# 96 dummy matmuls ahead of the first spectrum group, and two pieces of work moved from VectorE to ScalarE

**Chip, cores, metric.** The kernel runs on one core of a Trainium2 chip. The metric is the device time of one execution in microseconds (us); lower is better. Every run told of here was in the fast state: the granted clock was 0.998 to 1.0 throughout.

## The reference

Two layers alternate, A B A B, each in the form x + layer(layernorm(x)), on x of 2048 rows by 640 columns in bf16.

```python
def _A_ref(x, w_r, w_i):            # a filter in the spectrum
    X = rfft2(x.astype(float32))
    X = X * (w_r + 1j * w_i)
    return irfft2(X, s=(S, D)).astype(bfloat16)

def _B_ref(x, mem0, Wq, Wk, Wv, Wo, seg_len):   # 64 segments of 32 rows, 8 rows of memory carried on
    for s in range(n_seg):
        h = concatenate([mem, xs], axis=1)
        q, k, v = (einsum('btd,dhe->bhte', h, W) for W in (Wq, Wk, Wv))   # 32 heads of 128
        p = softmax(where(mask, einsum('bhqe,bhke->bhqk', q, k) * scale, -1e9))
        o = einsum('bhqk,bhke->bhqe', p, v)
        ...                                      # output projection; the first 8 rows become mem

x = x + _A_ref(_layernorm(x), A_w_r, A_w_i)
x = x + _B_ref(_layernorm(x), B_mem0, ...)
x = x + _A_ref(_layernorm(x), A_w_r, A_w_i)
x = x + _B_ref(_layernorm(x), B_mem0, ...)
```

## The kernel before

The change touches one function, which starts the first layer A from raw input. The 16 blocks of rows come in five loads and are worked on in five groups. For each row the moments are computed (on VectorE, or on ScalarE for rows 3, 7 and 11), then the row's factor (Ln and Exp on ScalarE, small operations on GpSimd). The layernorm isn't applied to the rows: the DFT table of the row is scaled instead. Then follow 60 matmuls a group (30 in the last two), five PSUM banks a group out of eight, and the evictions.

```python
groups = [(0, 4), (4, 8), (8, 12), (12, 14), (14, 16)]
by_act = (3, 7, 11)
pp = tc.alloc_tile_pool(name=f"{self.lname}_ps1", bufs=8, space=PSUM)

def act_stats(t):      # a row's moments on ScalarE
    nc.scalar.activation(out=scr[:, 0, :], in_=x[:, t, :], func=ACTF.Identity, scale=-D ** -1.5, accum_out=nm[:, t:t + 1])
    nc.scalar.activation(out=scr[:, 1, :], in_=x[:, t, :], func=ACTF.Square, scale=D ** -0.5, bias=nm[:, t:t + 1], accum_out=mv[:, t, 1:2])
...
def stats(t):          # the same on VectorE
    for hlf in range(2):
        nc.vector.bn_stats(out=st[:, t % 2, hlf, :], in_=x[:, t, hlf * 320:(hlf + 1) * 320])
    nc.vector.bn_aggr(out=mv[:, t, :], in_=st[:, t % 2, :, :])

def scale_tables(q):
    for t in range(*groups[q]):
        nc.vector.tensor_scalar_mul(out=Ts[:, t, :], in0=T[:, t, :], scalar1=rs[:, t:t + 1])
...
with tc.manual_schedule(...):      # every engine runs its part in the order written here
    ...
    empties(0, ps0, "  AAA")       # A: eviction on ScalarE, D: on VectorE
    for t in (12, 13):
        stats(t)
    scales(3)
    empties(1, ps1, "AA")
    scale_tables(2)
    ps2 = matmuls(2)
```

The reciprocals of the softmax sums go out to DRAM and come back broadcast to 128 partitions, two heads at a time. The value matmuls (`pso`) can run before that, but VectorE multiplies each finished bank by the broadcast (`Rb`) to empty it, and so frees the bank.

```python
def sums_back(h):
    ...
    nc.sync.dma_start(out=Rd[h][0:1, :].rearrange("o (g n) -> (o g) n", g=4), in_=R[0:128:32, :])
    if h % 2 or h == H - 2:
        for a in range(...):       # the pair's two heads
            nc.sync.dma_start(out=Rbs2[a % 2], in_=Rd[a][0:1, :].to_broadcast([128, 4 * NR]))

def value_group(h, P, Rb, oT, g_):
    pso = pa.tile([128, 512], FP32, name="pso", tag="pso")
    for ...:
        nc.tensor.matmul(pso[:, lo - q0:hi - q0], lhsT=V[...], rhs=P[...], ...)
    ...
    nc.vector.tensor_tensor(out=oT..., in0=byclass(po), in1=rx, op=ALU.mult)
    nc.vector.tensor_tensor(out=oTm[:, h, ...], in0=po[:, :, SEG], in1=rm, op=ALU.mult)
```

Of the kernel before, what the change touches and what calls it, by code (L numbers as in the profile page):

```python
# [10 lines left out]
FP32 = mybir.dt.float32  # L11
# [6 lines left out]
DRAM = bass.MemoryType.DRAM  # L18

S, D = 2048, 640  # L20
NF = 321
LN_EPS = 1e-5

# [171 lines left out]
class LayerA:  # L195
# [8 lines left out]
    def tables(self, gate=None, mirror=True):  # L204
        nc, cd = self.tc.nc, self.g["cd"]
        s5 = self.ar.get("S5", f"{self.lname}tab")
        self.Fd = s5.bf(5, 2, NF)
        self.K = s5.bf(19, 128)
        self.Wm = s5.bf(2, 7 * NF)
        self.wts = [s5.bf(2, NF) for _ in range(3)]  # L210
        self.W = {}
# [10 lines left out]
    def load_mirror(self, i):  # L222
        self.tc.nc.gpsimd.indirect_dma_start(out=self.Wm[:, i, :], out_offset=None, in_=self.w[i].rearrange("(p g) f -> p (g f)", g=16),
                                             in_offset=bass.IndirectOffsetOnAxis(ap=self.g["mirror"][:, 0:1], axis=0), element_offset=9 * NF)

    def load_w(self, p):
        nc, W, j = self.tc.nc, self.W, self.SEQ[p]
        W[j, 0] = self.wts[p % 3]
        if j:
            W[j, 1] = self.Wm[:, :, (7 - j) * NF:(8 - j) * NF]  # L230
        for i in range(2):
# [35 lines left out]
    def cold_raw(self, x_src, s3):  # L267




        nc, tc, g, x, T = self.tc.nc, self.tc, self.g, self.x, self.T
        Ts, scr = s3.bf(16, 128), s3.bf(2, D)
        mh = s3.bf(16, 2)
        st, mv = s3.f32(2, 2, nc.vector.BN_STATS_DIM), s3.f32(16, 2)
        nm, mn, rs, r0 = (s3.f32(16) for _ in range(4))
        for a, b in ((0, 2), (2, 4), (4, 8), (8, 12), (12, 16)):
            nc.sync.dma_start(out=x[:, a:b, :], in_=r16(x_src)[:, a:b, :])
            if a in (4, 8):
                nc.sync.dma_start(out=T[:, 2 * a - 8:2 * a, :], in_=g["cd"]["cT"][:, 2 * a - 8:2 * a, :])  # L280
        groups = [(0, 4), (4, 8), (8, 12), (12, 14), (14, 16)]
        by_act = (3, 7, 11)
        pp = tc.alloc_tile_pool(name=f"{self.lname}_ps1", bufs=8, space=PSUM)

        def act_stats(t):
            nc.scalar.activation(out=scr[:, 0, :], in_=x[:, t, :], func=ACTF.Identity, scale=-D ** -1.5, accum_out=nm[:, t:t + 1])
            nc.scalar.activation(out=scr[:, 1, :], in_=x[:, t, :], func=ACTF.Square, scale=D ** -0.5, bias=nm[:, t:t + 1], accum_out=mv[:, t, 1:2])

        def scales(q):
            a, b = groups[q]  # L290
            sl, v = slice(a, b), mv[:, a:b, 1]
            small = nc.gpsimd if q < 4 else nc.vector
            nc.scalar.activation(out=r0[:, sl], in_=v, func=ACTF.Ln, bias=g["eps"][:, 0:1])
            nc.scalar.activation(out=r0[:, sl], in_=r0[:, sl], func=ACTF.Exp, scale=-0.5)
            n = b - 1 if b - 1 in by_act else b
            small.tensor_scalar_mul(out=mn[:, a:n], in0=mv[:, a:n, 0], scalar1=-1.0)
            if n < b:
                small.tensor_scalar_mul(out=mn[:, n:b], in0=nm[:, n:b], scalar1=D ** 0.5)
            t, r = rs[:, sl], r0[:, sl]
            if small is nc.gpsimd:  # L300
                small.tensor_scalar_add(out=t, in0=v, scalar1=LN_EPS)
                small.tensor_tensor(out=t, in0=t, in1=r, op=ALU.mult)
            else:
                small.scalar_tensor_tensor(out=t, in0=v, scalar=LN_EPS, in1=r, op0=ALU.add, op1=ALU.mult)
            small.tensor_tensor(out=t, in0=t, in1=r, op=ALU.mult)
            small.tensor_scalar(out=t, in0=t, scalar1=-0.5, scalar2=1.5, op0=ALU.mult, op1=ALU.add)
            small.tensor_tensor(out=t, in0=t, in1=r, op=ALU.mult)
            small.tensor_copy(out=mh[:, sl, 0], in_=mn[:, sl])
            small.tensor_tensor(out=mh[:, sl, 1], in0=mn[:, sl], in1=mh[:, sl, 0], op=ALU.subtract)

        def stats(t):
# [3 lines that stand above are left out]

        def scale_tables(q):
            for t in range(*groups[q]):
                nc.vector.tensor_scalar_mul(out=Ts[:, t, :], in0=T[:, t, :], scalar1=rs[:, t:t + 1])

        def matmuls(q):  # L320
            a, b = groups[q]
            ps = {}

            def rows(ch):
                ps[ch] = pp.tile([128, 4, 128], FP32, name="ps1", tag="pa")
                for t in range(a, b):
                    nc.tensor.matmul(ps[ch][:, t - a, :], lhsT=x[:, t, ch * 128:(ch + 1) * 128], rhs=Ts[:, t, :], start=(t == a), stop=False)

            def means(ch):
                for t in range(a, b):  # L330
                    for i in range(2):
                        nc.tensor.matmul(ps[ch][:, t - a, :], lhsT=mh[:, t, i:i + 1].to_broadcast([128, 128]), rhs=Ts[:, t, :], start=False, stop=(i == 1 and t == b - 1))  # L332

            for ch in range(5):
                rows(ch)
                if ch > 1:
                    means(ch - 2)
            means(3)
            means(4)
            return ps  # L340

        def empties(q, ps, by):
            for ch, e in enumerate(by):
                if e != " ":
                    self.empty(nc.vector.tensor_copy if e == "D" else nc.scalar.copy, ps[ch], ch, *groups[q])
        with tc.manual_schedule(engines={nc.tensor.engine, nc.scalar.engine, nc.vector.engine, nc.gpsimd.engine}):
            act_stats(3)
            for t in (0, 1, 2):
                stats(t)
            scales(0)  # L350
            self.tables(mirror=False)
            self.load_mirror(0)
            act_stats(7)
            for t in (4, 5):
                stats(t)
            scale_tables(0)
            ps0 = matmuls(0)
            stats(6)
            scales(1)
            self.load_mirror(1)  # L360
            act_stats(11)
            for t in (8, 9):
                stats(t)
            scale_tables(1)
            empties(0, ps0, "AA")
            ps1 = matmuls(1)
            stats(10)
            scales(2)
            empties(0, ps0, "  AAA")
            for t in (12, 13):  # L370
                stats(t)
            scales(3)
            empties(1, ps1, "AA")
            scale_tables(2)
            ps2 = matmuls(2)
            stats(14)
            stats(15)
            scale_tables(3)
            scales(4)
            empties(1, ps1, "  AAA")  # L380
            ps3 = matmuls(3)
            scale_tables(4)
            empties(2, ps2, "AAADD")
            empties(3, ps3, "AADAD")
            ps4 = matmuls(4)
            empties(4, ps4, "DADAD")
        pp.release()
# [9 lines left out]
    def spectrum(self, late_loads=(), handoff=None):  # L397
# [3 lines left out]
        s1 = self.ar.get("S1", f"{self.lname}tmp")  # L401
        quads = [s1.bf(4, NF) for _ in range(5)]
        ts = [[s1.f32(2, 2, NF) for _ in range(2)] for _ in range(2)]
# [1405 lines left out]
```

## Time and profile before

| | before |
|---|---|
| time | 1562.96 us, median of 3 (1561.68 to 1563.09) |
| profiled span | 1561.0 us |
| PE busy | 1532.8 us, 98%, 14,482 matmuls |
| first real matmul | 10.08 us |
| spectrum starts (line 427) | 26.99 us |

PE is the bound, so a gain must be an earlier matmul, and the place to look is PE's idle time. The lines for the start stand in the prediction.

### The profile page before, as it was taken

Reading aid. Unit: us, or ns where it says so; the run is one execution under the profiler, and the core shown is the slowest. Engines: PE = TensorE matmul, PEld = TensorE weight load, DVE = VectorE, ACT = ScalarE, POOL = GpSimd, SP = SyncE. Lnnn points to the kernel's source line nnn. Section 1 sums busy time; section 2 is a strip of 40 time slices with the busy share of each in tenths; the row PEclk is TensorE's granted clock in tenths of the full one; section 3 lists DMA queues with packets and bytes.
Section 4 is the critical chain, followed back from the end, with each engine's and each line's share of the span. In section 5 each row is a group of like instructions: output and inputs, shape, how many; then the busy total and the mean of one; then the engine's idle time right before and its main releaser. Section 6 shows DMA issues by size and latency. Waiting matters only on the chain.

```text
span 1561.0 us, 36510 instructions
## 1 busy us (share of the span) xinstructions
PE 1532.8 (98%) x14482; PEld 1078.2 (69%) x14483; DVE 807.2 (52%) x2414; ACT 771.6 (49%) x2251; POOL 234.4 (15%) x327
## 2 busy tenths in 40 slices
PE   7999999999999999999999999999999999999998
PEld 6776666666666666677777766666666666666776
DVE  6873545555455555633367545655455545553111
ACT  5584555556555565511136655556555565562000
POOL 3520111112111121100034101112111121110000
PEclk9999999999999999999999999999999999999999
DMA  4681344334433444636114514343433434327242
GB/s 170 219 304 31 110 147 144 137 134 139 158 132 137 150 125 151 190 105 184 51 49 156 185 51 143 137 142 131 167 128 139 151 121 174 124 99 230 68 128 65
DMA packets 159764, 214.86 MB, mean 138 GB/s; under 512 B 7136, under 2 KB 133096, under 8 KB 151648
## 3 DMA queue, kind: packets, MB, share of 16 engines
q1 hardware_dynamic: 159008, 210.14, 40.9%
q8 instruction: 115, 1.88, 0.5%
q0 software_dynamic: 576, 2.30, 0.5%
q14 instruction: 65, 0.53, 0.1%
HBM read 167.32 MB, written 45.10 MB: 136 GB/s over the span
## 4 chain that ended last, share of the span: by engine, by line
PE 91%; DMA 3%; DVE 2%; ACT 2%; issue 1%; POOL 0%; SPq 0%; DVEq 0%; ACTq 0%; POOLq 0%
PE psk L1135 18%; PE psv L1201 18%; PE psx L1480 17%; PE psq L1135 17%; PE pso L1284 4%; PE pss L1211 4%; PE ab L427 2%; DMA bB_S<-Rd 2%; PE psg L585 1%; PE psl L1238 1%; PE psq L1159 1%; PE X L458 1%; PE psu L519 1%; PE psm L911 1%; PE ps L332 1%
## 5 line engine op out<-in xcount | busy, mean ns | idle before, releaser
L1135 PEld LDWEIGHTS <-bB_S 128*128 128x128 bf16 x3180 | 261.4, 97 | 181.1 <-DMA bB_S<-in_B_Wk_dram 1.1
L1194 DVE CAST bB_S<-psk 128x495 bf16<-128x495 f32 (+3 forms) x320 | 191.6, 599 | 276.7 <-PE psk L1135 272.2
L1480 PE MATMUL psx<-Wo_sb,bB_S 128*128 128x320 bf16 x2048 | 288.3, 299 | 0.1
L1214 ACT ACTIVATE bB_S<-pss 128x269 bf16<-128x269 f32 (+5 forms) x576 | 208.9, 386 | 139.8 <-PE pss L1211 139.5
L1480 PEld LDWEIGHTS <-bB_S 128*128 128x128 bf16 x2048 | 196.9, 98 | 74.1 <-DVE bB_S L1298 0.7
L1179 ACT ACTIVATE bB_S<-psq 128x96 bf16<-128x96 f32 x300 | 152.1, 507 | 174.1 <-PE psq L1135 174.1
L1298 DVE TENSOR_TENSOR bB_S<-pso,bB_S 128x480 bf16<-128x480 f32 (+1 forms) x320 | 192.8, 603 | 79.7 <-DMA bB_S<-Rd 52.8
L1254 POOL TENSOR_TENSOR bB_S<-bB_S,bB_S 128x535 f32<-128x535 f32 x90 | 111.6, 1253 | 797.9 <-DVE bB_S L1246 762.9
L1215 DVE TENSOR_TENSOR bB_S<-bB_S,maskf 128x269 bf16<-128x269 bf16 (+5 forms) x576 | 158.9, 289 | 109.1 <-ACT bB_S L1214 109.1
L1203 ACT CAST bB_S<-psv 128x512 bf16<-128x512 f32 (+1 forms) x288 | 162.4, 564 | 80.9 <-PE psv L1201 80.9
L1201 PE MATMUL psv<-bB_S,B1hT_S 128*128 128x256 bf16 x1360 | 168.8, 272 | 0.0
L1201 PE MATMUL psv<-bB_S,B2hT_S 128*128 128x256 bf16 x1360 | 168.8, 272 | 0.0
L1135 PE MATMUL psk<-B2hT_S,bB_S 128*128 128x495 bf16 (+3 forms) x800 | 164.2, 343 | 0.0
L1135 PE MATMUL psk<-B1hT_S,bB_S 128*128 128x495 bf16 (+3 forms) x800 | 164.2, 343 | 0.0
L1135 PE MATMUL psq<-B1hT_S,bB_S 128*128 128x495 bf16 (+5 forms) x780 | 156.1, 336 | 0.6 <-DMA bB_S<-in_B_Wk_dram 0.5
L1135 PE MATMUL psq<-B2hT_S,bB_S 128*128 128x495 bf16 (+5 forms) x780 | 156.1, 336 | 0.5 <-DMA bB_S<-in_B_Wk_dram 0.5
L1201 PEld LDWEIGHTS <-B2hT_S 128*128 128x128 bf16 x1360 | 129.8, 98 | 24.4
L1201 PEld LDWEIGHTS <-B1hT_S 128*128 128x128 bf16 x1360 | 129.8, 98 | 24.4
L1211 PE MATMUL pss<-bB_S 128*128 128x132 bf16 (+8 forms) x1152 | 137.5, 219 | 0.0
L1211 PEld LDWEIGHTS <-bB_S 128*128 128x128 bf16 x1152 | 95.5, 97 | 55.3
L1284 PE MATMUL pso<-bB_S,bB_S 128*128 128x132 bf16 (+8 forms) x1152 | 118.7, 219 | 4.4 <-DVE oTmf L1301 4.3
L1284 PEld LDWEIGHTS <-bB_S 128*128 128x128 bf16 x1152 | 89.3, 98 | 37.6 <-DVE oTmf L1301 6.9
(293 smaller groups left out, 1424.8 us busy)
## 6 DMA issues: line engine op xcount, KB each, us to landing
bB_S<-Rd SPq DMA_DIRECT2D x62, 1070.0 KB
oTx_d<-bB_S SPq DMA_DIRECT2D x60, 512.0 KB
bB_S<-oTx_d SPq DMA_DIRECT2D x46, 512.0 KB
bB_S<-in_B_Wq_dram SPq DMA_DIRECT2D x32, 320.0 KB
bB_S<-in_B_Wk_dram SPq DMA_DIRECT2D x32, 320.0 KB
bB_S<-in_B_Wv_dram SPq DMA_DIRECT2D x32, 320.0 KB
Wo_sb<-in_B_Wo_dram SPq DMA_DIRECT2D x4, 1280.0 KB
B1wv_S<-in_B_Wv_dram SPq DMA_DIRECT2D x10, 512.0 KB
```

Source lines behind the costliest of these rows:

```text
L1135: nc.tensor.matmul(ps, lhsT=w[:, ch, hh * 128:(hh + 1) * 128], rhs=src[:, ch, lo:hi], start=(ch == 0), stop=(ch == 4))
L1179: nc.scalar.mul(out=qv[:, :, 0:SEG], in_=x_view(ps, o, n)[:, :, 1:SW], mul=scale)
L1194: nc.vector.tensor_copy(out=KTs[h % 2][:, lo:hi], in_=ps[:, 0:hi - lo])
L1201: nc.tensor.matmul(ps[:, i * 256:(i + 1) * 256], lhsT=hT[:, ch, st.hcol((t + i) * 128):st.hcol((t + i) * 128) + 128], rhs=w["Wv"][:, ch, : ...
L1203: nc.scalar.copy(out=V[:, t:t + n, :].rearrange("p a b -> p (a b)"), in_=ps[:, 0:n * 256])
L1211: nc.tensor.matmul(ps[:, off - o0:off - o0 + hi - lo], lhsT=KT[:, t * 128:(t + 1) * 128], rhs=QT[:, lo:hi], start=True, stop=True)
L1214: nc.scalar.activation(out=E[:, 0:n], in_=ps[:, 0:n], func=ACTF.Exp)
L1215: nc.vector.tensor_tensor(out=P[:, o0:o0 + n], in0=E[:, 0:n], in1=bs.mask[:, o0:o0 + n], op=ALU.mult)
L1254: nc.gpsimd.tensor_tensor(out=acc, in0=acc, in1=part, op=ALU.add)
L1284: nc.tensor.matmul(pso[:, lo - q0:hi - q0], lhsT=V[:, t, (h % 2) * 128:(h % 2 + 1) * 128], rhs=P[:, off:off + hi - lo], start=(i == 0), st ...
L1298: nc.vector.tensor_tensor(out=oT.rearrange("p (r s j) -> p r s j", r=16, j=2)[:, :, s0:s0 + ns, :], in0=byclass(po), in1=rx, op=ALU.mult)
L1480: self.tc.nc.tensor.matmul(ps[:, 0:320], lhsT=lhs(h, k // 2), rhs=self.g["Wo_sb"][:, h, c0:c0 + 320], start=(h == 0), stop=(h == H - 1))
```

## The change

The intent: in the profile of before, a matmul of 128 columns took 106 ns until 15.9 us and 56 ns after that (the lines are in the prediction), so the whole of group 0 ran slow. 96 dummy matmuls on a tile of ones, issued as soon as that tile is written, should release the clock before group 0's data are there. That matmuls ahead would do this was the author's assumption; the clock records of before show the release at 15.87 us. Group 0's tables are scaled on ScalarE, so that they are there sooner and VectorE is freed, and row 13's moments go from VectorE to ScalarE for the same reason.

```diff
+WARM = 96
...
-        by_act = (3, 7, 11)
+        by_act = (3, 7, 11, 13)
         pp = tc.alloc_tile_pool(name=f"{self.lname}_ps1", bufs=8, space=PSUM)
+        idle = pp.tile([128, 4, 128], FP32, name="idle", tag="pa")
+        for i in range(WARM):
+            nc.tensor.matmul(idle[:, i % 4, :], lhsT=g["ones"][:], rhs=g["ones"][:], start=True, stop=True)
...
         def scale_tables(q):
             for t in range(*groups[q]):
-                nc.vector.tensor_scalar_mul(out=Ts[:, t, :], in0=T[:, t, :], scalar1=rs[:, t:t + 1])
+                if q:
+                    nc.vector.tensor_scalar_mul(out=Ts[:, t, :], in0=T[:, t, :], scalar1=rs[:, t:t + 1])
+                else:
+                    nc.scalar.mul(out=Ts[:, t, :], in_=T[:, t, :], mul=rs[:, t:t + 1])
...
-            for t in (12, 13):
-                stats(t)
+            stats(12)
+            act_stats(13)
```

## The prediction

> **What bounds the kernel now.** The page's busy table shows PE busy 98% of 1561.0 us, so a change to the first 27 us matters only through the moment at which the matmuls behind it can start. I first asked what PE waits for:
>
> ```profile
> PE ps L327 <- DVE A1xn_S L318: 10.1, 1, 10.1
> PE pso L1284 <- DVE oTmf L1301: 4.3, 5, 1.1
> PE ab L427 <- DVE A1YT_S L265: 0.5, 1, 0.5
> ```
>
> The longest wait is the start: PE does nothing for 10.08 us, until VectorE has scaled the first table of group 0 (line 318). Next, the chain of work that ended last, in order of time:
>
> ```profile
> 10.08 1.61 PE ps L327 x12
> 11.68 0.85 PE ps L332 x8
> ...
> 14.24 2.17 PE ps L332 x24
> 16.42 0.67 PE ps L327 x12
> 17.09 0.45 PE ps L332 x8
> ...
> 26.50 0.44 DVE A1YT_S L265
> 26.99 2.93 PE ab L427 x20
> ```
>
> From 10.08 to 26.46 the chain is PE alone, and the spectrum stage (line 427) starts at 26.99 after a last eviction. The same eight matmuls cost 0.85 us at 11.68 and 0.45 at 17.09: 106 ns each, then 56. The counts by microsecond show when that changes (columns: stretch, length, PE, PEld, DVE, ACT, POOL busy with counts, PE clock, DMA share, GB/s):
>
> ```profile
> 15.00:16.00 1.00, 1.00 (x13) 1.00 (x12) 0.93 (x4) 0.43 (x3) 0.61 (x3) 1.00 1.02 379
> 16.00:17.00 1.00, 1.00 (x22) 1.00 (x20) 0.96 (x4) 1.00 (x4) 0.70 (x4) 1.00 1.09 322
> ```
>
> A matmul that overlaps a stretch counts in it, so 13 and 22 overstate the rates, but the jump falls at about 15.9, 5.8 us after the first matmul (the clock column says 1.00 throughout and doesn't show it). All 60 matmuls of group 0 ran slow, 6.34 us (10.08 to 16.42); each later group of 60 took 3.35. Last, ScalarE in the same stretch:
>
> ```profile
> 11.64 0.30 ACT L293 ACTIVATE A1xn_S<-A1xn_S,eps 128x4 f32<-128x4 f32 x1 [2.20 <-DVE A1xn_S L314]
> 15.53 0.30 ACT L293 ACTIVATE A1xn_S<-A1xn_S,eps 128x4 f32<-128x4 f32 x1 [0.73 <-DVE A1xn_S L314]
> 18.07 1.05 ACT L265 CAST A1YT_S<-ps 128x512 bf16<-128x512 f32 x2
> 20.35 0.29 ACT L293 ACTIVATE A1xn_S<-A1xn_S,eps 128x2 f32<-128x2 f32 x1 [1.23 <-DVE A1xn_S L314]
> 20.78 3.64 ACT L265 CAST A1YT_S<-ps 128x512 bf16<-128x512 f32 x8
> ```
>
> Its whole slack between 9.5 and 24.4 us is 2.20 + 0.73 + 1.23 = 4.2 us, and at the end it runs eight evictions without a gap. That is where the added work goes.
>
> [...]
>
> **The change part by part.**
>
> 1. 96 dummy matmuls. They need only the ones tile (written by 1.09), so PE starts near 1.15. [...] Gain on group 0 alone: 60 x 50 ns = 3.0 us.
>
> 2. Scaling of group 0 on ScalarE. VectorE loses four operations, 9.78 to 10.43 plus a start slot: its next moments (row 6) start at 9.78 instead of 10.43, 0.65 earlier. ScalarE can start when row 7's moments are done, 9.35, as GpSimd has the factors by 9.21. [...] PE starts real work at 9.80, and ends group 0 near 10.68 + 56 x 0.056 = 13.8 instead of 16.42.
>
> 3. Group 1. Row 6's moments, ScalarE's Ln/Exp and GpSimd's chain of small operations all shift by 0.62, so VectorE's tables start at 13.03 instead of 13.65, and its first is out at 13.28. PE follows at 13.8 and ends near 17.1, instead of 19.77: 2.7 us ahead.
>
> 4. Group 2's tables. Row 10's moments end at 14.82, GpSimd's factors come at 16.88 (17.50 less 0.62), tables from 16.92. First matmul at about 17.2, 2.4 us ahead of 19.60 in the timeline. On PE alone it would end at 20.8.
>
> 5. Row 13's moments on ScalarE. They take 1.78 us (7.66 to 9.44 for row 7) and stand between the evictions of group 0's channels 2-4 and the Ln/Exp of group 3, which precedes the evictions of group 1's channels 0 and 1. ScalarE: Ln of group 2 at 14.91 (15.53 less 0.62), three evictions 15.36 to 16.78 (0.47 each), row 13 to 18.55, Ln/Exp of group 3 to 19.1, then the two evictions from 19.02: done at 19.59 and 20.08. Before, they were done at 18.64 and 19.12. So they come 1.0 us LATER, while PE wants them 2.1 us earlier. With eight banks, group 2's channel 3 reuses the bank of group 1's channel 0. PE gets there at 17.2 + 0.5 + 16 x 0.056 = 18.6, and stops until 19.65. Then 40 matmuls remain: group 2 ends at 21.9 (before: 23.12).
>
> 6. Groups 3 and 4. ScalarE's evictions resume at 20.41 (Ln/Exp of group 4 from 19.97), against 20.78: only 0.37 ahead. Group 3 (30 matmuls) starts at 21.9, waits 0.15 for group 2's channel 1 (evicted by 22.9), ends near 23.75. Group 4 ends near 25.4 (before 26.46). The last eviction still takes 0.53, so line 427 starts near 25.9, against 26.99.
>
> Sum: 3.0 us freed on PE in group 0; 0.3 more from the earlier start; less about 1.0 of waiting for tables in groups 0 to 2, 1.0 for the bank of group 2's channel 3, and about 0.2 for later banks. Left: 1.1 us. Behind 27 us the chain is PE with work gated on it; its one long transfer (4.74 us from 112.09) is issued after the computed rows are stored, so it moves along. The gain passes to the end: 1562.96 - 1.1 = 1561.9. I lean 0.1 lower, as the bank wait is the least certain term: 1561.8.
>
> **The rivals.**
>
> A. PE is the bound throughout, no bank wait. For: today's chain there is pure PE, and no wait is visible between 10 and 26 us. Against: that is because slow group 0 lets everyone else get ahead. Then only the tables delay it: group 2 ends at 20.8, group 3 at 22.5, group 4 at 24.2, and the spectrum starts at 24.7. Gain 2.3 us, 1560.7.
>
> B. ScalarE bounds the whole stage, no gain. [...] An eviction 0.5 us later than I have it, or a late table, leaves 0.5 us: 1562.5.
>
> C. The warm-up fails: the clock isn't released, or dummies hold PE beyond 9.8. All 96 slow would end at 11.4 and cost PE 1.3 us more than the 10.08 of today: 1562.5 to 1564. [...]
>
> D. The clock's phase. In the profile of before it was released late. [...] The three runs spread 1.4 us (1561.68 to 1563.09), which may be this. A median taken with lucky phases would shrink my gain to about 0.5.
>
> **Range and chances.** The mechanism leaves 0.5 to 2.3 us of gain and the runs of before alone spread 1.4: 1560.3 to 1562.9 should hold it 8 times in 10. Two per cent is 31 us; the whole stage touched is 27 us long. Within 2%: 0.99, the rest half each for something unseen.
>
> **What would show it.** In the profile after: matmuls from about 1.15 us[...]; real group 0 from 9.8, all at 56 ns; group 2's first matmul near 17.2; a PE wait of about 1 us on a ScalarE eviction near 18.6 to 19.7; row 13's moments near 16.8 to 18.6 on ScalarE; line 427 starting near 25.9. No PE wait there and a start near 24.7 would prove rival A; a start after 26.5, B; slow matmuls after 9.8, C. If line 427 starts 1 us earlier but the end does not, the claim that the rest only follows is wrong.

The traces show this instead. In before, the spacing of the matmuls goes from 107 to 56 ns at 15.87 us, 5.8 us after the first. If dummies from 1.15 take as long, 54 of them run slow and 42 fast, and the last ends near 9.3, ahead of 9.80 (an estimate from these numbers). A table took 386 ns on ScalarE, 291 apart (after). That a gap before group 0 would not lose the clock was not shown. Nor was it shown that the clock has a phase, as rival D supposes; "released late" can be read as 5.8 us after group 0's first matmul in before, against 4.1 in e2 (13.78 less 9.71).

## More of the kernel before

One part of the profile's page, which the prediction didn't use, becomes important, the DMA queues (columns: queue and kind; packets, MB, share of the time of 16 engines):

```profile
q1 hardware_dynamic: 159008, 210.14, 40.9%
q8 instruction: 115, 1.88, 0.5%
```

The second queue carries no data of the kernel. Each of its 115 packets has exactly 16,384 bytes in the trace, and against PE's instructions (14,482 matmuls and 14,483 weight loads are counted) they come, from the 4th packet to the 113th, one every 255.7 PE instructions on average. So I take it that this queue brings PE its own instructions, 256 to a packet (an estimate from these counts); such a packet is called a refill below.

## The result

The changed kernel takes 1559.65 us (median of 6, 1559.56 to 1560.40); the kernel before, timed beside it, 1561.98 us (median of 6, 1560.64 to 1563.09). The ratio is 0.9986, 95% interval 0.9973 to 0.9999. A ratio is the mean time of one kernel's fast runs over that of the other's of the same rounds, so not quite the ratio of the medians quoted. The gain of 2.3 us is twice what I predicted, and 1559.65 lies below the range of 1560.3 to 1562.9. The profiled spans are 1557.9 and 1561.0, 3.1 us apart.

**The first 27 us went as predicted.** PE's timeline of the changed kernel (start, length, engine, line, what; in brackets the idle time before and what ended it):

```profile
1.14 7.56 PE L287 MATMUL idle<-ones 128*128 128x128 bf16 x96 [1.14 <-DVE ones L1698]
10.12 1.54 PE L334 MATMUL ps<-A1xn_S,A1x_S 128*128 128x128 bf16 x12 [1.41 <-ACT A1xn_S L325]
11.49 0.61 PE L339 MATMUL ps<-A1xn_S 128*128 128x128 bf16 x8
...
17.57 1.06 PE L334 MATMUL ps<-A1xn_S,A1x_S 128*128 128x128 bf16 x12
18.47 0.61 PE L339 MATMUL ps<-A1xn_S 128*128 128x128 bf16 x8
19.92 0.38 PE L334 MATMUL ps<-A1xn_S,A1x_S 128*128 128x128 bf16 x4 [0.85 <-ACT A1YT_S L266]
```

The dummies end at 8.70; the trace's clock records put the release of the clock at 5.44, and the spacing of the dummies falls to 56 ns at 5.47. Real work starts at 10.12 and is fast, with matmuls 55 to 56 ns apart once the four tables are there. Group 2 starts at 17.57, runs twelve matmuls on rows and eight on their means, then stops for 0.85 us for a bank that ScalarE must empty. ScalarE's timeline shows why:

```profile
9.68 1.26 ACT L325 ACTIVATE A1xn_S<-A1xn_S 128x128 bf16<-128x128 bf16 x4
...
17.03 0.76 ACT L290 ACTIVATE A1xn_S<-A1x_S 128x640 bf16<-128x640 bf16 x1
...
17.92 0.83 ACT L291 ACTIVATE A1xn_S<-A1x_S,A1xn_S 128x640 bf16<-128x640 bf16 x1
...
19.31 1.06 ACT L266 CAST A1YT_S<-ps 128x512 bf16<-128x512 f32 x2
```

The four tables take 1.26 us, row 13's moments stand at 17.03 to 18.8, and the evictions follow at 19.31. The spectrum starts at 26.40, 0.59 us earlier than before. Part of the missing gain is chance: the load of rows 4 to 7 landed 0.33 us later in this execution. Over the 14 profiles row 4's moments began anywhere between 7.01 and 8.49 us. Counted from that moment, the stage took 19.25 us before and 18.33 after, a gain of 0.92.

**The other 2.5 us came behind 27 us, where nothing was changed.** I paired each of the 14,482 real matmuls of the two traces and followed the lead of the changed kernel: 0.58 us at 27 us, 0.87 from 117 us, 1.57 from 334.6, 2.32 from 624.6, 2.98 from 1390.3, 3.06 at the end. The three large steps (0.7, 0.7 and 0.5 us) fall on value matmuls of layer B. PE's waits of the changed kernel (waited for: us in total, times, longest):

```profile
PE pso L1291 <- DVE oTmf L1308: 2.3, 3, 1.1
PE ps L334 <- ACT A1xn_S L325: 1.4, 1, 1.4
PE idle L287 <- DVE ones L1698: 1.1, 1, 1.1
...
PE ps L334 <- ACT A1YT_S L266: 0.8, 1, 0.8
```

The first line was 4.3 us in five waits before: 2.0 us of the gain. One by one, the five were 0.54 us at 334.6, 1.00 at 624.6, 1.02 at 646.3, 0.64 at 1390.3 and 1.08 at 1412.1. The ones at 646.3 and 1412.1 follow the last broadcast of a layer and are there in all 14 traces, about 1.0 to 1.15 us each; in place of the other three the changed kernel has 0.25 and 0.10. (The 10.1 us wait of before for the first table has become the second and third line, with the dummies between.) Here is one of those places, the timeline of the kernel before around 334.6 us:

```profile
325.78 1.46 SPq L1268 DMA_DIRECT2D bB_S<-Rd  x2
...
333.77 0.66 DVE L1298 TENSOR_TENSOR bB_S<-pso,bB_S 128x480 bf16<-128x480 f32 x1 [3.17 <-DMA bB_S<-Rd]
...
334.64 0.41 PE L1284 MATMUL pso<-bB_S,bB_S 128*128 128x132 bf16 x4 [0.54 <-DVE oTmf L1301]
```

and the same head pair in the changed kernel:

```profile
324.92 1.45 SPq L1275 DMA_DIRECT2D bB_S<-Rd  x2
...
331.68 0.66 DVE L1305 TENSOR_TENSOR bB_S<-pso,bB_S 128x480 bf16<-128x480 f32 x1 [1.94 <-DMA bB_S<-Rd]
```

From the issue of the broadcast to the first product on VectorE: 333.77 - 325.78 = 7.99 us before, 331.68 - 324.92 = 6.76 us after. The late one leaves no free bank, and PE waits 0.54 us. VectorE's total wait for broadcasts is a bad guide to this: it is 52.8 us before and 60.1 us after, because most of it is slack, and because some of these waits are put down to another engine (27 waits are listed before, 32 after). What reaches PE is read from PE's own waits.

What else moved in the two stretches? The DMA queues of the kernel before, 325.8 to 333.8 us:

```profile
q1 hardware_dynamic: 270, 2.09, 68.6%
q8 instruction: 1, 0.02, 1.8%
```

and of the changed kernel, 324.9 to 331.7 us:

```profile
q1 hardware_dynamic: 208, 1.58, 60.3%
```

In the late one, a refill came in beside the broadcast. Its one packet took 1.8% of 16 engines' 8.0 us, which is 2.3 us; the mean of all 115 is 0.5% of 16 x 1561 us, shared out, 1.1 us. If a refill is 256 PE instructions (the mean distance is 255.7 in both traces), adding 2 x 96 = 192 ahead of everything moves every later refill against the code by 192 modulo 256. The traces agree: with the 192 taken off, a refill of after stands 192 PE instructions ahead of the next one of before (median). Behind the first stage the two traces show no other difference: the instructions of every engine, and the DMA issues, come in the same order.

This gave the theory to test, **F**: the position of PE's refills (the number of PE instructions added ahead, modulo 256) decides how many broadcasts are late; position 0 is as before, position 192 as after. The rival, **S**: a start some tenths of a microsecond earlier, or the moved work, is what makes the difference.

### The profile page after: what moved, and what is told of

It reads as the page before. It is cut to its first block, busy times and chain, and to the rows that moved or that the text cites. A ratio compares the mean times of both kernels' runs of the same rounds, so it can differ in the third digit from the quotient of the medians.

```text
span 1557.9 us, 36704 instructions
## 1 busy us (share of the span) xinstructions
PE 1538.1 (99%) x14578; PEld 1083.2 (70%) x14579; DVE 805.4 (52%) x2407; ACT 774.7 (50%) x2259; POOL 234.5 (15%) x328
## 4 chain that ended last, share of the span: by engine, by line
PE 91%; DMA 3%; DVE 2%; ACT 2%; issue 1%; POOL 1%; SPq 0%; DVEq 0%; ACTq 0%; POOLq 0%
PE psv L1208 18%; PE psk L1142 18%; PE psx L1487 17%; PE psq L1142 17%; PE pso L1291 4%; PE pss L1218 4%; PE ab L434 2%; DMA bB_S<-Rd 2%; PE psg L592 1%; PE psl L1245 1%; PE psq L1166 1%; PE X L465 1%; PE psu L526 1%; PE psm L918 1%; DMA bB_S<-in_B_Wk_dram 1%
## 5 line engine op out<-in xcount | busy, mean ns | idle before, releaser
L1305 DVE TENSOR_TENSOR bB_S<-pso,bB_S 128x480 bf16<-128x480 f32 (+1 forms) x320 | 193.1, 603 | 75.3 <-DMA bB_S<-Rd 60.1
```

The costliest lines, as they stand in the source:

```text
L1305: nc.vector.tensor_tensor(out=oT.rearrange("p (r s j) -> p r s j", r=16, j=2)[:, :, s0:s0 + ns, :], in0=byclass(po), in1=rx, op=ALU.mult)
```

## The experiments

All kernels gave correct results. They ran in three calls on chips of the same kind: e1 to e4, e5 to e8, e9 to e12; each call has nine runs of the kernel before, with medians 1561.44, 1561.94 and 1561.68. One run varies by 1 to 2 us and the intervals of a ratio are about 2 us wide each way, so no single comparison below decides; what decides is how the kernels group, and the profiles. "Rest" is the profiled span less the start of the spectrum, thus all that the change doesn't touch. "Waits" are PE's on a bank of `pso`.

| kernel | added | position | time us | ratio [95%] | spectrum at | rest | waits us, times |
|---|---|---|---|---|---|---|---|
| before | 0 | 0 | 1561.98 | | 26.99 | 1534.0 | 4.3, 5 |
| after | 192 | 192 | 1559.65 | 0.9986 [0.9973, 0.9999] | 26.40 | 1531.5 | 2.3, 3 |
| e1, 128 dummies | 256 | 0 | 1561.45 | 1.0003 [0.9989, 1.0016] | 26.29 | 1533.4 | 3.3, 4 |
| e2, 96 tiny dummies alone | 192 | 192 | 1560.61 | 0.9999 [0.9985, 1.0013] | 26.14 | 1531.7 | 2.5, 3 |
| e3, dummies alone | 192 | 192 | 1559.66 | 0.9989 [0.9976, 1.0003] | 25.94 | 1531.9 | 2.8, 4 |
| e4, moves alone | 0 | 0 | 1561.94 | 1.0003 [0.9989, 1.0017] | 27.17 | 1532.9 | 3.5, 4 |
| e5, row 13 on VectorE | 192 | 192 | 1559.74 | 0.9985 [0.9971, 0.9998] | 26.55 | 1532.3 | 2.9, 4 |
| e6, after again | 192 | 192 | 1560.14 | 0.9989 [0.9976, 1.0003] | 26.21 | 1532.2 | 2.7, 4 |
| e7, e6 + 32 tiny | 256 | 0 | 1561.69 | 0.9996 [0.9983, 1.0010] | 26.34 | 1533.6 | 4.0, 4 |
| e8, e6 + 64 tiny | 320 | 64 | 1563.21 | 1.0013 [0.9999, 1.0026] | 26.28 | 1534.4 | 3.7, 6 |
| e9, e6 + 128 tiny | 448 | 192 | 1562.98 | 1.0006 [0.9992, 1.0020] | 29.68 | 1531.9 | 2.5, 3 |
| e10, e5, longer dummies | 192 | 192 | 1559.92 | 0.9988 [0.9974, 1.0001] | 26.47 | 1531.7 | 2.7, 4 |
| e11, e3 again | 192 | 192 | 1560.10 | 0.9987 [0.9973, 1.0001] | 26.52 | 1532.2 | 2.8, 4 |
| e12, after, third time | 192 | 192 | 1560.26 | 0.9990 [0.9976, 1.0003] | 26.54 | 1531.8 | 2.7, 4 |

(Times are medians of 5 runs, 6 for the first two.)

### e1: one whole block of instructions

```diff
-WARM = 96
+WARM = 128
```

> The changed kernel with 128 dummies instead of 96. In the two profiles the changed kernel starts the spectrum stage (line 427 before, 434 after) only 0.59 us earlier, yet ends 3.1 us earlier: the rest comes in steps inside layer B, where PE waits for the broadcast of the reciprocal sums (4.3 us in five waits before, 2.3 in three after). Theory F: those waits depend on where PE's instruction fetches fall. The instruction queue q8 moved 115 packets, 1.88 MB, so about 16 KB each; [...] 96 dummies, a weight load and a matmul each, are 192 instructions and move the fetches against the code by three quarters of a block; 128 dummies are 256 and put them back where they were before. So F expects: stage as in the changed kernel (line 434 near 26.4), PE's waits on line 1308 back at 3.5 to 4.5 us, time 0.6 to 1.0 us under before. Rival G (the rest is chance from run to run): time as the changed kernel, 2.2 us under before.

Measured: 1561.45, against 1561.44 for the kernel before; rest 1533.4, waits back at 3.3 us (3.5 to 4.5 expected). Group 0 ran fast, its 60 matmuls in 3.35 us (10.81 to 14.16), but the longer dummies held PE until 10.81. The gain is gone as F says; of the small gain that F left to the stage, nothing is seen in the time.

### e2: the instructions without their work

On the kernel before, with nothing moved:

```diff
+        for i in range(WARM):
+            nc.tensor.matmul(idle[0:1, i % 4, 0:1], lhsT=g["ones"][:, 0:1], rhs=g["ones"][:, 0:1], start=True, stop=True)
```

> Before plus 96 dummies of one column by one column: the same 192 PE instructions, hardly any work, nothing moved to ScalarE. Theory F: the start stays cold (group 0 about 6.3 us, line of the first ab matmul near 27.0 us), but layer B's waits fall to about 2 us: time 1.2 to 1.8 us under before. Rival G: as before within 0.5 us. If even these dummies release the clock, matmuls after 10 us will be 56 ns apart, and the run says nothing on its own.

Measured: these 96 take 2.54 us in all and didn't bring the release forward to group 0's start: it came at 13.78, in the midst of group 0. The profile fits F: rest 1531.7, 2.5 us of waits. The time fits it half at most: 1560.61, which is 0.8 us under before by medians, 0.5 by means and 0.2 by the ratio, instead of 1.2 to 1.8, with runs from 1559.55 to 1562.21. By its time alone, e2 doesn't show that the position acts without a warm start. The profiled run is the fastest of the five; what the slow ones did I can't see.

### e3 and e11: the dummies alone

The changed kernel with the tables and row 13 back on VectorE.

```diff
-        by_act = (3, 7, 11, 13)
+        by_act = (3, 7, 11)
...
-                if q:
-                    nc.vector.tensor_scalar_mul(out=Ts[:, t, :], in0=T[:, t, :], scalar1=rs[:, t:t + 1])
-                else:
-                    nc.scalar.mul(out=Ts[:, t, :], in_=T[:, t, :], mul=rs[:, t:t + 1])
+                nc.vector.tensor_scalar_mul(out=Ts[:, t, :], in0=T[:, t, :], scalar1=rs[:, t:t + 1])
...
-            stats(12)
-            act_stats(13)
+            for t in (12, 13):
+                stats(t)
```

> Before plus the 96 dummies, tables of group 0 and row 13 left on VectorE. By the arithmetic of the prediction: PE starts group 0 at 10.1, fast, waits for the tables of groups 1 and 2 (13.7 and 17.5), and in group 3 for banks that ScalarE empties from 20.8 on: spectrum starts near 26.3, 0.6 to 0.7 us before the kernel before, that is, as much as the whole change. With F the end is then about 2 us under before, within 0.4 us of the changed kernel; if the moves to ScalarE matter it ends over 0.7 us later than the changed kernel.

> The dummies alone again, beside the changed kernel on the same chip: whether the two moves to ScalarE are worth anything. By the arithmetic before (spectrum 0.6 us under the kernel before in both): within 0.3 us of the changed kernel. If the moves are part of the gain: over 0.5 us above it.

Measured: 1559.66 and 1560.10; the whole change gave 1559.65, 1560.14 and 1560.26. So the dummies alone have the whole gain in time, to within what these runs resolve. In the stage, counted from row 4's moments, the moves are worth a little: 18.83 and 18.57 us without them, 18.33, 18.34 and once 19.20 with them.

### e4: the moves alone

```diff
-        idle = pp.tile([128, 4, 128], FP32, name="idle", tag="pa")
-        for i in range(WARM):
-            nc.tensor.matmul(idle[:, i % 4, :], lhsT=g["ones"][:], rhs=g["ones"][:], start=True, stop=True)
```

> The changed kernel without dummies. Group 0 runs slow again (about 6 us from 10.1), PE is the bound to the end of the stage, spectrum starts within 0.4 us of the kernel before; PE's instruction positions are those of before, so with F layer B's waits stay near 4 us: time within 0.5 us of before. If the moves were worth something by themselves it would end more than 0.7 us under before.

Measured: 1561.94, rest 1532.9, waits 3.5 us: nothing gained. Without the dummies the stage takes 19.53 us from row 4's moments, no less than the 19.25 of before.

### e5: the bank wait taken away

```diff
-        by_act = (3, 7, 11, 13)
+        by_act = (3, 7, 11)
...
-            stats(12)
-            act_stats(13)
+            for t in (12, 13):
+                stats(t)
```

> The changed kernel with row 13's moments back on VectorE (dummies and ScalarE tables kept). VectorE idles 0.93 us before the tables of group 2 in the changed kernel's profile, and the row's moments are about 1.0 us there, so the tables come at most 0.2 later; ScalarE loses 1.8 us just ahead of the evictions for which PE waited 0.85 us. My theory of the bank wait: the 0.8 us wait on ScalarE (line 334 on 266 in the changed kernel) goes, spectrum starts 0.5 to 0.9 us earlier relative to the first load, time 1558.8 to 1559.2. PE instructions stand as in the changed kernel, so layer B as there. Rival: later banks take the wait over and the time stays at 1559.6.

Measured: the 0.85 us wait is gone, which shows that row 13's moments on ScalarE caused it. PE's timeline shows the largest wait left between 12 and 26 us:

```profile
22.44 0.27 PE L334 MATMUL ps<-A1xn_S,A1x_S 128*128 128x128 bf16 x2 [0.22 <-ACT A1YT_S L266]
```

Yet the stage became only 0.27 us shorter (18.06 against 18.33): later evictions and the end of the stage take most of it back. The time, 1559.74 against e6's 1560.14 (means 0.5 apart), goes the right way, but less than I expected and less than these runs resolve.

### e6 and e12: the changed kernel again

No edit; e6 is the standard for e5, e7 and e8, and e12 for e9 to e11.

> The changed kernel again, for the same chip: 1559.3 to 1560.0, about 2 us under before; layer B's waits about 2.3 us in three. If it comes out within 0.7 us of before, the gain itself is chance and theory G stands.

> The changed kernel for this chip: 1559.5 to 1560.4, 1.2 to 2.2 us under before; layer B's waits 2 to 3 us; whether the clock is kept between the dummies and group 0 decides on the spectrum's start by about 0.3 us only, as the bank wait swallows the rest.

Measured: 1560.14 and 1560.26, rest 1532.2 and 1531.8: the result repeats, but smaller. Against before the gain is 1.8 and 1.4 us by medians, where it was 2.3 at first. e6 showed something new. PE's timeline:

```profile
1.15 7.05 PE L287 MATMUL idle<-ones 128*128 128x128 bf16 x96 [1.15 <-DVE ones L1698]
9.70 1.54 PE L334 MATMUL ps<-A1xn_S,A1x_S 128*128 128x128 bf16 x12 [1.50 <-ACT A1xn_S L325]
...
12.23 1.06 PE L339 MATMUL ps<-A1xn_S 128*128 128x128 bf16 x8
```

Eight matmuls of means took 1.06 us, where the first profile after had 0.61. The counts by stretch of the same kernel (stretch, length, PE, PEld, DVE, ACT, POOL busy with counts, granted clock, DMA share, GB/s) show the cause in the clock column:

```profile
8.00:10.00 2.00, 0.43 (x6) 0.19 (x4) 1.93 (x7) 1.97 (x7) 1.57 (x9) 1.00 1.02 413
10.00:12.00 2.00, 1.84 (x21) 1.60 (x21) 1.93 (x6) 1.94 (x7) 1.72 (x4) 0.80 1.06 401
12.00:14.00 2.00, 2.00 (x22) 2.00 (x20) 1.17 (x7) 1.69 (x4) 1.52 (x7) 0.50 1.01 416
14.00:15.00 1.00, 1.00 (x16) 1.00 (x14) 0.93 (x4) 0.04 (x1) 0.69 (x2) 0.69 1.02 407
```

Here the clock was released early (4.38), the dummies ended at 8.20, and after a gap of 1.5 us the first 12 matmuls came at the pace of the tables. Then the clock fell: it was half from 11.20 to 14.62. The stage took 19.20 us. So 96 dummies don't hold the clock in every execution; it was lost in e11 too (11.85 to 15.26) and in e9 (from 13.99). In all three the fall comes 6.83 us after the release, twice the 3.41 us for which the clock then stays down. If time is counted in stretches of 3.41 us from the release, the second stretch held 19 matmuls of 128 columns in e6 and 23 in e11 (a full stretch later on holds 61), and in e9 one-column ones almost alone; it held 26 or more in the eight other kernels with dummies of full size, and all eight kept the clock. That the clock is decided by such stretches is read off these traces, not tested. It cost e6 little at 26.21 only because its first load was early (row 4's moments began at 7.01).

### e7: 64 PE instructions more, and nothing else

The cleanest test: e6 with 32 tiny dummies behind the others, 0.94 us of PE in the gap where it is idle anyway.

```diff
+        for i in range(32):
+            nc.tensor.matmul(idle[0:1, i % 4, 0:1], lhsT=g["ones"][:, 0:1], rhs=g["ones"][:, 0:1], start=True, stop=True)
```

> The changed kernel with 32 further dummies of one column: 256 PE instructions in all ahead of group 0, as in the run with 128 dummies, but done before group 0 can start (26 ns each in the run with 96 small ones, under 1 us). Theory F: stage exactly as in the changed kernel, layer B's waits as in before (3.3 to 4.3 us), time 1.2 to 1.8 us over the changed kernel of this call. Rival G: as the changed kernel. Rival H (the 128 dummies lost time because they held PE until 10.8): as the changed kernel too.

Measured: the stage is that of the changed kernel (18.35 us from row 4's moments, spectrum at 26.34), but the time is 1561.69, 1.55 us over e6 (1.2 by the means). No run of e7 is below 1561.19, while four of e6's five are below 1560.2. PE's waits of e7:

```profile
PE pso L1293 <- DVE oTmf L1310: 4.0, 4, 1.1
```

and of e6:

```profile
PE pso L1291 <- DVE oTmf L1308: 2.7, 4, 1.1
```

The broadcast shown above for before and after is late again in e7, 332.30 - 325.15 = 7.15 us, with a refill beside it, but there PE doesn't wait for it. Pairing the matmuls of e6 and e7 shows where the time goes: e7 loses 0.73 us at 622 us and 0.59 at 1388, most of the 1.55 us between the two profiles, and both are value matmuls behind a late broadcast. The first place in e7 (the broadcast's issue, the refill in 614.9 to 622.3, PE's wait):

```profile
614.95 1.97 SPq L1277 DMA_DIRECT2D bB_S<-Rd  x2
q8 instruction: 1, 0.02, 0.8%
623.19 0.41 PE L1293 MATMUL pso<-bB_S,bB_S 128*128 128x132 bf16 x4 [0.98 <-DVE oTmf L1310]
```

and in e6, with no packet of q8 in 614.6 to 621.3:

```profile
614.58 1.43 SPq L1275 DMA_DIRECT2D bB_S<-Rd  x2
622.10 0.41 PE L1291 MATMUL pso<-bB_S,bB_S 128*128 128x132 bf16 x4 [0.25 <-DVE oTmf L1308]
```

From issue to first product the broadcast took 7.37 us in e7 and 6.65 in e6. All other engines and the DMA issues have the same order in both traces, so the refills of other engines (q14: 65 packets) can't be the difference. S falls: the start is as early, the moved work is there, and the gain is gone.

### e8: a third position

As e7, with `range(64)`.

> The changed kernel with 64 further small dummies: 320 instructions, a quarter of a fetch block past the position of before. F says that the time depends on the position, not on how many dummies there are: broadcasts issued within some 2.5 us ahead of a fetch come late, others not, and the fetches move some 3.4 us (a quarter of about 13.8 us between them). A fetch at 1.9 us after the issue in before goes to about -1.5, those at 8.3 and 9.5 to about 4.9 and 6.1, so I expect few late broadcasts and a time within 0.6 us of the changed kernel. G and H: as the changed kernel as well. A loss of over 1 us would mean that any added dummy costs, and speak against F.

Measured: missed. At 1563.21, 3.07 us over e6, it is the slowest of all; rest 1534.4. The refills fall 5.3 to 6.1 us after the issue of some broadcasts, and I had taken that as harmless; two of those broadcasts took 7.9 us. Paired with e6, the profile of e8 loses 0.6 us behind each of these two, at 300 and 1067 us, and 1.2 us near 880. There PE's waits list one that no other kernel has, on nothing that the profile shows:

```profile
PE pso L1293 <- DVE oTmf L1310: 3.7, 6, 1.1
...
PE psvb L1582 <- issue: 1.1, 1, 1.1
```

### e9: a full block more than the changed kernel

As e7, with `range(128)`: 256 instructions more, so the position of the changed kernel again.

> The changed kernel with 128 further small dummies, one whole fetch block of PE instructions more than it has. Theory F (position): layer B's fetches stand against the code as in the changed kernel, so no late broadcasts 1 to 2.6 us after their issue, and the time is that of the changed kernel of this call within 0.5 us, though 32 more cost 1.5 us and 64 more 3.4 us over it in the last two profiles and times. Theory H2 (each added dummy costs): 3 to 7 us over it. Group 0 starts up to 2 us later (128 x 26 ns behind the last full dummy), which the bank wait of 0.85 us and the table waits should swallow but for some tenths.

Measured: the time missed, 1562.98, but not for the reason under test. The tiny dummies ran until 14.0 us, 0.9 us of it waiting for issue, so real work began late; the clock was lost at 13.99; and the spectrum began at 29.68, 3.2 us late. The rest is 1531.9 us, and PE's waits are those of the changed kernel:

```profile
PE pso L1293 <- DVE oTmf L1310: 2.5, 3, 1.1
```

1562.98 less 3.2 is 1559.8. F holds in the part that it speaks of.

### e10: the best version I could put together

e5 (no bank wait), with the last six dummies four times as long to keep the clock:

```diff
-        for i in range(WARM):
+        for i in range(WARM - 6):
             nc.tensor.matmul(idle[:, i % 4, :], lhsT=g["ones"][:], rhs=g["ones"][:], start=True, stop=True)
+        for i in range(6):
+            nc.tensor.matmul(idle[:].rearrange("p a b -> p (a b)"), lhsT=g["ones"][:], rhs=g["ones"][:, 0:1].to_broadcast([128, 512]), start=True, stop=True)
```

> Row 13 on VectorE, 90 dummies of 128 and 6 of 512 columns: the same number of PE instructions, but PE is busy 1 us longer (6 times 160 ns more), so the gap ahead of group 0, in which the second run of the changed kernel lost its clock at 11.2 us, is shorter. I expect the clock kept, no bank wait over 0.3 us, spectrum start 18.0 to 18.3 us after row 4's moments begin, and a time 0.2 to 0.6 us under the changed kernel of this call. If the bank wait and the lost clock are worth nothing: within 0.2 us of it.

Measured: the six long dummies took 1.47 us in all (8.31 to 9.78), the clock was kept (group 0's matmuls of means took 0.61 us for eight), the gap before real work was 0.7 us, no bank wait over 0.2 us, and the stage took 18.05 us. The time, 1559.92, is 0.3 us under e12, both by medians and by means. That is within the noise, and not shown to be better.

### All traces together

Over the 14 traces I sorted 420 broadcasts (30 head pairs each) by when a refill of instructions began relative to them, and took the time from issue to the first product on VectorE:

| start of the refill, us after the broadcast's issue | broadcasts | mean us | over 6.85 us |
|---|---|---|---|
| none between -3 and 6.5 | 279 | 6.63 | 2, longest 6.88 |
| -3 to -1 | 64 | 6.64 | 2, longest 6.98 |
| -0.2 to 0.6 | 31 | 6.99 | 16 |
| 0.6 to 1.5 | 22 | 6.93 | 10 |
| 1.5 to 2.7 | 14 | 7.22 | 12, longest 7.99 |
| 5 to 6.5 | 10 | 6.90 | 2, longest 7.91 |

At position 0 every third head pair has its refill 1.0 to 2.6 us after the broadcast's issue; the exception is the last pair of the first layer, the one at 616 us, with -0.1 to 0.5. At position 192 the refill comes 1.8 to 1.0 us ahead, where 2 of 64 broadcasts are late by a little, or at -0.1 to 0.5, where about half are late.

Counted by trace: at position 0, 6 or 7 of the 30 head pairs took over 6.9 us, together 3.6 to 4.5 us more than 6.63 each; at position 192, 0 to 4 did, together at most 2.3 us more. Not each of them reaches PE: most of its waits are behind the last broadcasts of a layer. Behind the last pair of each layer (issued near 616 and 1382 us) the wait follows the broadcast: 7.0 to 7.4 us from issue to product go with 0.6 to 1.0 us of waiting, 6.5 to 6.9 with at most 0.5; and only at position 0 does a refill fall between 0.1 us before and 6.5 after the issue of these pairs.

The rest of the kernel's time grows with what a trace's late broadcasts took beyond 6.63 us in sum: 1531.5 to 1531.8 us in the four traces where it is at most 0.5 us, 1531.9 to 1532.3 in the five with 1.3 to 2.3, and 1532.9 to 1534.0 in the four with 3.6 to 4.5 (e8, with 2.5 us and its other wait, stands apart at 1534.4). The last four are the profiles at position 0 (mean 1533.5), the other nine those at position 192 (mean 1531.9): no overlap, 1.6 us apart. The times group likewise: 1561.44 to 1561.98 for all seven medians at position 0 (four of them of the kernel before), 1559.65 to 1560.61 for the eight at position 192 without e9.

That the position decides is shown by the grouping, in which the two positions don't overlap, and by e7 against e6, where nothing else differs. That it acts through broadcasts that meet a refill is what the traces show side by side; no run delays a broadcast in another way. Why a packet of 16 KB delays a transfer of 1070 KB by up to 1.4 us isn't shown; the profile has no view of the order inside a DMA engine. An estimate gives the usual size: a packet of the broadcast has 8,560 bytes and took 324 ns (median, before), so 16,384 bytes at that rate are about 0.6 us of one DMA engine. At the peak 17 to 20 packets of a broadcast are under way at a time (12 on average, before), and its last packet decides when it has landed; if one engine's share comes 0.6 us later, so does the whole.

## Why the prediction was wrong

The prediction's number missed by 2.15 us (1561.8 against 1559.65), but 1.0 of this lies in its base: it counted from 1562.96, the median of three runs, and the kernel before came out at 1561.98 over six. The gain itself was 2.3 us instead of 1.2. Step by step:

1. *Dummies from 1.15*: right (1.14). The times for the release and the last dummy were 5.44 and 8.70. That the gap before group 0 would be too short to lose the clock held in the first profile (no fall before 1555.1), but not in general: e6 lost it, at 11.20, after a gap of 1.5 us followed by thinly spread matmuls.
2. The tables' cost on ScalarE: 386 ns each, 291 apart. *Real work at 9.80*: 10.12, as the load came 0.33 us later.
3. and 4. *Group 2's first matmul at 17.2*: 17.57, the same shift.
5. *A bank wait of about 1 us from row 13's moments*: right, 0.85 us, and e5 removed it by removing the cause.
6. *Spectrum at 25.9, stage gain 1.1*: 26.40 and 0.59 in the two profiles; 0.92 counted from row 4's moments. The mechanism was right and the size 0.2 us off, besides the chance of the load.
7. *"Behind 27 us the chain is PE with work gated on it ... it moves along. The gain passes to the end"*: this step failed. Behind 27 us the changed kernel gained more than it did in the stage: 2.5 us in the two profiles, and 1.6 us between the groups of profiles at positions 0 and 192. The 192 PE instructions ahead move PE's instruction refills away from layer B's broadcasts, and waits of 4.3 us become 2.3. I had looked at one long transfer behind the stage, and at none of the five waits for `pso`, though their line stood second in the first view that I quoted. I had also followed the chain that ended last to 120 us only: over the whole span of before it runs through five broadcasts, issued at 325.78, 616.29, 638.62, 1382.38 and 1404.31, of 6.7 to 7.8 us each. The claim that the work behind moves along has no place for a transfer whose length depends on where a refill falls.

The sum as measured: 1.6 us from the position, and 0.2 to 0.7 from the start being warm. The latter is from medians: at position 0, e1 and e7 average 1561.57 against 1561.76 for the four of before; at position 192, the seven warm kernels average 1559.92 against e2's 1560.61. Together 1.8 to 2.3; measured 2.3 in the first, 1.8 and 1.4 in the two repeats, so part of the first 2.3 may be chance. The moves to ScalarE add nothing measurable (e3 and e11 against after, e6, e12; e4 against before).

Of the rivals, A (no bank wait, gain 2.3) gives the measured gain for a wrong reason: the bank wait was there, and the spectrum started at 26.40, not 24.7. Had I judged by the gain alone, I'd have taken it for proven. C and D are partly real: in some executions the clock does decide whether group 0 is fast (released at 13.78 in e2, half from 11.20 to 14.62 in e6), but the time hardly shows it.

Open: why e2 has only half of the expected gain in time; what the wait for issue near 880 us is that cost e8 1.2 us; and whether another position is better still, since only 0, 64 and 192 were tried.

## What to carry to other kernels

A change of a few tenths of a per cent in a long kernel may come from where its instructions lie, not from what they do (here 1.6 us of 1560). Pair the same instruction in both traces and look where the lead grows; if it grows in code that wasn't touched, add idle instructions until the count is back at the old place, modulo a refill of the instruction queue (255.7 PE instructions here), and time that too. And "the rest only follows" is a claim about waits far from the change: name the waits that PE has there before resting a sum on it.
